# Second-layer weight blocks nine and ten of a fused attention and two-layer kernel: converted in other stretches of the program

## The chip, the cores and the metric

One core of a Trainium2 chip runs the whole program. The metric is the device time of an execution in microseconds (us). PE is the engine for matrix products, DVE the vector engine, ACT the engine for activation functions, POOL the general engine (GpSimd), and SP the engine whose queue issues nearly all DMA transfers.

## What is computed

Block-causal attention, a first layer with h - tanh(h), and a second, gated layer with a norm ahead of it, all in float32:

```python
attn = softmax(mask(q @ k.T / sqrt(64)))            # 4 x 8 heads x 576 x 64, blocks of 64
x = (attn @ v).transpose(0, 2, 1, 3).reshape(2304, 512)
h = x @ w_in                                        # 512 -> 2048
x = (h - tanh(h)) @ w_out                           # 2048 -> 512
xn = x / sqrt(mean(x * x) + 1e-6) * rms_g
g, val = xn @ w_gate, xn @ w_val                    # 512 -> 1536 each
out = (g / (1 + exp(-g)) * val) @ w_out2            # 1536 -> 512
```

## The kernel before, in words

The 2304 tokens are worked in six groups of 384. Attention and the first layer run interleaved, group by group (g = 0 to 5, 16 steps j each); the last group has no attention left, so its place beside the first layer is taken by preparing the second layer. The second layer then runs in three passes, each over a pair of groups. In a pass, `fast` (line 1095) goes through the 12 blocks j of the gate and value weights, 128 columns each. Per block PE forms seven products of six matmuls, in the order 1, 4, 5, 6, 0, 3, 2, so 42 matmuls; DVE adds and multiplies their results (lines 1112, 1113, 1115, 1117, 1121, 1122), ACT takes c (line 1111) and the silu (lines 1116, 1118), POOL one product (line 1119). Line 1121 takes product 2, the block's last. Then follow the products with the output weights.

Float32 numbers are multiplied as a high and a low part, each in a reduced format. So every weight block has to be **converted** before use (class `Convert`, line 776). A block's weights are two pieces (gate and value) of 512 KB. `load` brings a piece from memory into a staging tile `st` (SP); `piece` turns it into float32 in a tile `fu` (two ACT steps `cv`, `cu`, lines 141 and 143, and two DVE steps, lines 144 and 145; inputs arrive as float64 words). The seven weight combinations of the seven products are then made and split. The first half, combinations 0 to 2, is split as it stands: ACT writes the high part (line 803), DVE the low part (line 108), 768 columns. Four POOL sums (lines 794 to 798) then change `fu` in place, so they wait for the first split; then the second half, combinations 3 to 6, is split, 1024 columns. `fill` splits into `ws`, the tile that PE reads; `send` splits into a passing tile `wc` and stores it to memory (`w2d` for gate blocks, `wod` for output blocks). A block that was filled is stored too (`keep`), for passes two and three. `ws` has three buffers.

Where the blocks are converted: the six output blocks in groups three to five (g = 2 to 4), by a list of 24 items (`away`, line 828, four items a block) from which a number of items is taken after each step (line 996). In the last group a second list of 24 items: blocks 10, 0, 11, 1, 2 in full, of which 0, 1 and 2 stay in `ws`, and the two pieces of blocks 3 and 4. In pass one blocks 3 to 9 (`WHOLE`, line 52) are filled: 3 and 4 from their finished pieces, 5 to 9 from the start. In the loop over j, at block j the second half of block j + 1 is filled (line 1276), the first half of block j + 2 (line 1080, through `load_slot`), and the pieces of blocks j + 3 and j + 4 are converted (lines 1283 to 1286). Blocks 10 and 11 come back from `w2d` by a load, and in passes two and three all blocks do.

What sets the order: the PE queue is in the order in which the code is written. The order of DVE, ACT, POOL and SP is set by a scheduler when the program is built, up to the first block after `WHOLE`; from there on DVE, ACT and POOL too keep the written order (line 1273). Each engine works through its queue in that order.

Of the kernel before, what the change touches and what calls it, by code (L numbers as in the profile page):

```python
# [26 lines left out]
J1 = FF1 // 128  # L27
J2 = FF2 // 128
# [20 lines left out]

EARLY = 4  # L50
JH = J2 // 2
WHOLE = range(3, 10)
LAG = 2
SPLIT = 12
AVLEAD = 3
# [39 lines left out]
def build(ctx, tc, q, k, v, w_in, w_out, w_gate, w_val, w_out2, rms_g, ident_in, out):  # L95
# [496 lines left out]
    with tc.manual_schedule(engines={PE.engine}):  # L592
# [13 lines left out]
        class Both:  # L606
            n = 0
# [220 lines left out]
        def away(units, stay=(), raw=()):  # L828

            items = []  # L830
            fourth = None
            for n, c in enumerate(units):
                def first(n=n, c=c):
                    if n == 0:
                        c.load()
                    c.piece(0)
                    if n + 1 < len(units):
                        units[n + 1].load((0,))

                def second(n=n, c=c):  # L840
                    c.piece(1)
                    if n + 1 < len(units):
                        units[n + 1].load((1,))

                def third(c=c):
                    if c in stay:
                        c.fill(slot(c.j), 0)
                        return
                    c.send(0)
                    c.sums()  # L850

                def last(c=c):
                    if c in stay:
                        c.fill(slots[c.j], 1)
                    else:
                        c.send(1)
                items += [first, fourth, second] if fourth else [first, second]
                fourth = None
                if c not in raw:
                    items.append(third)  # L860
                    fourth = last
            return items + ([fourth] if fourth else [])
# [27 lines left out]
        def pair_x():  # L890
            return [[(wk if n == 0 else tp).tile([128, 4 if n < 3 else 2, TG], F32R, name=f"x{y}{n}",
                                                 tag=f"x{y}" if n == 0 else f"x{y}{n}") for y in "hl"] for n in range(4)]
# [16 lines left out]
        def slot(q):  # L909
            slots[q] = tp.tile([128, 2, 7, 256], F32R, name="ws", tag="ws", bufs=3)  # L910
            return slots[q]

        items = away([Convert("o", j) for j in range(JH)])
        x = None

        PREP = [(1, lambda: pair_load(0, 0)), (1, lambda: pair_load(0, 1)), (1, lambda: rms(0, 12)),
# [11 lines left out]
        for s in range(NSA):  # L928
            g, j = divmod(s, J1)
# [58 lines left out]
            if len(pend) > LAG:  # L988
                n = pend.pop(0)
# [3 lines left out]
                    out1(n, t)  # L993
                gts.pop(n)
            if 2 <= g < NG - 1:
                nit = {2: 0, 3: 5, 4: 13}[g] + max(j - 2, 0) * {2: 5, 3: 8, 4: 13}[g] // (J1 - 3)
                while 4 * JH - len(items) < min(nit, 4 * JH):
                    items.pop(0)()
            if j == J1 - 1:
                while att.pos < goal:  # L1000
                    att.step()
                if g == NG - 2:
                    mid.__exit__(None, None, None)
                    evm.__exit__(None, None, None)
                    cvs.__exit__(None, None, None)
                    x4.__exit__(None, None, None)
                    sat.close()
                    sw = ExitStack()
                    tp = sw.enter_context(tc.tile_pool(name="w2p", bufs=1, side="right"))
                    sw0 = ExitStack()  # L1010
                    env["cvp"] = sw0.enter_context(tc.tile_pool(name="w0", bufs=1, side="right"))
                    env["stg"] = sw0.enter_context(tc.tile_pool(name="st2", bufs=2, side="right"))
                    sev = ExitStack()
                    ev = sev.enter_context(tc.tile_pool(name="ev", bufs=3, side="right"))
                    space = tp.tile([128, 2, 7, 256], F32R, name="ws", tag="ws", bufs=3).bitcast(F32)
                    space = space.rearrange("p x n c -> p (x n c)")
                    env["x2s"] = lambda g, t: (space[:, DM * t:DM * t + DM] if g == NG - 2 else
                                               ev.tile([128, DM], F32, name="x2s", tag="x2s"))
                    x = pair_x()
                    wcp = sev.enter_context(tc.tile_pool(name="wcp", bufs=1, side="right"))  # L1020
                    env["wc"] = lambda: wcp.tile([128, 2, 4, 256], F32R, name="wc", tag="wc")
                    direct = [Convert("g", j) for j in range(J2)]
                    items = away([direct[n] for n in (10, 0, 11, 1, 2, 3, 4)], direct[0:3], direct[3:5])
            if g == NG - 1:
                for k, f in PREP:
                    if k == j:
# [46 lines left out]
        def load_slot(q):  # L1073
# [4 lines left out]
            if j < J2:  # L1078
                if p == 0 and j in WHOLE:
                    direct[j].fill(w, 0)  # L1080
# [189 lines left out]
        for p in range(NG // 2):  # L1270
            for j in range(J2):
                if p == 0 and j == WHOLE.stop:
                    ordered.enter_context(tc.manual_schedule(engines={DVE.engine, ACT.engine, POOL.engine}))
                if p == 0:
                    if j + 1 in WHOLE:
                        direct[j + 1].fill(slots[j + 1], 1)
                    if j + 1 < WHOLE.stop:
                        direct[j + 1].keep()
                if p or j:
                    load_slot(p * NQ + j + 2)  # L1280
                if p == 0:
                    if 5 <= j + 3 < WHOLE.stop:
                        direct[j + 3].piece(1)
                    if 5 <= j + 4 < WHOLE.stop:
                        direct[j + 4].load()
# [4 lines left out]
                for t in range(2):  # L1290
                    n = j - t - (8 if p == 0 else 7)
# [35 lines left out]
```

## Time and profile before

| | us |
|---|---|
| median of 3 runs | 1016.61 (1016.61 to 1017.07) |
| the profiled execution's own time | 1016.32 |
| its span, first to last instruction | 1014.5 |
| PE busy in the span | 1000.3 |
| first layer's last group ends, pass one begins | about 602 |
| the first-layer group before the last ends, staging of the last group begins | about 520 |

The span is read from its first to its last instruction; the execution's own time is 1.8 us more. [...] A matmul of 384 columns starts 0.17 us after the one ahead of it, though its row gives it about 0.34 us: matmuls overlap, so a busy PE can hide a gap of up to 0.17 us, and waits are read from one start to the next.

### The profile page before, as it was taken

The numbers are of one execution on the slowest core, as the hardware profiler recorded it, in microseconds if no ns is written. First come the engines' busy times: TensorE is split into PE (matmuls) and PEld (weight loads), VectorE is DVE, ScalarE is ACT, GpSimd is POOL, SyncE is SP. The second block draws the span as 40 slices with busy tenths as digits, with TensorE's granted clock in tenths as the row PEclk, the third lists the DMA queues.
The fourth block names the chain that finished last, engine by engine and source line by source line (L and its number), as shares of the span: only waits on it lengthen the run. The fifth ranks groups of instructions, "written<-read, shape, count | busy, mean of one in ns | idle before, by whom it ended". The sixth has DMA issues, their size and how long they took to land.

```text
span 1014.5 us, 17814 instructions
## 1 busy us (share of the span) xinstructions
PE 1000.3 (99%) x5983; PEld 921.8 (91%) x5983; DVE 705.6 (70%) x1497; ACT 659.5 (65%) x1530; POOL 341.9 (34%) x474
## 2 busy tenths in 40 slices
PE   8999999999999999999999999999999999999998
PEld 5766789999999999999899889999999999999998
DVE  6977867876777677687657887966854458644565
ACT  6978978887888778697858675635632247412253
POOL 5522112322323242434333424575121470111710
PEclk9999999999999999999999999999999999999999
DMA  9899959865787689867869998987796667876664
GB/s 225 252 352 341 282 170 263 270 195 143 207 252 206 181 241 287 231 204 240 301 208 363 377 345 317 353 310 278 278 350 254 249 228 257 298 284 233 257 219 156
DMA packets 185419, 265.22 MB, mean 261 GB/s; under 512 B 109040, under 2 KB 150384, under 8 KB 178032
## 3 DMA queue, kind: packets, MB, share of 16 engines
q1 hardware_dynamic: 184240, 263.69, 79.2%
q8 instruction: 47, 0.77, 0.3%
q10 hardware_dynamic: 1088, 0.39, 0.2%
q14 instruction: 44, 0.36, 0.1%
HBM read 201.65 MB, written 62.39 MB: 260 GB/s over the span
## 4 chain that ended last, share of the span: by engine, by line
PE 78%; DVE 6%; ACT 3%; issue 2%; POOL 2%; DMA 1%; SPq 0%; DVEq 0%; ACTq 0%; POOLq 0%
PE t L715 5%; PE t L717 5%; PE t L716 5%; PE gv L1064 5%; PE gv L1062 5%; PE t L481 5%; PE gv L1063 5%; PE acc L750 4%; PE acc L748 4%; PE acc L749 4%; PE t L525 3%; PE ga L1064 3%; PE ga L1062 3%; PE ga L1063 3%; PE ga L748 3%; PE ga L750 2%
## 5 line engine op out<-in xcount | busy, mean ns | idle before, releaser
L715 PE MATMUL t<-xh,w 128*128 128x384 f32 x384 | 138.6, 361 | 0.2
L717 PE MATMUL t<-xh,w 128*128 128x384 f32 x384 | 130.0, 339 | 0.4 <-DVE w L108 0.2
L716 PE MATMUL t<-xl,w 128*128 128x384 f32 x384 | 129.3, 337 | 0.0
L1064 PE MATMUL gv<-xh,ws 128*128 128x384 f32 x322 | 108.4, 337 | 3.2 <-DVE ws L108 3.2
L1062 PE MATMUL gv<-xh,ws 128*128 128x384 f32 x322 | 108.2, 336 | 0.2 <-DVE vb L1115 0.2
L1063 PE MATMUL gv<-xl,ws 128*128 128x384 f32 x322 | 108.1, 336 | 0.0
L748 PE MATMUL acc<-w,gh 128*128 128x512 f32 x252 | 102.5, 407 | 0.0
L750 PE MATMUL acc<-w,gl 128*128 128x512 f32 x252 | 99.7, 395 | 0.4 <-DVE gl L108 0.3
L749 PE MATMUL acc<-w,gh 128*128 128x512 f32 x252 | 99.2, 393 | 0.0
L1119 POOL TENSOR_TENSOR g<-va,vb 128x384 f32<-128x384 f32 x36 | 37.0, 1027 | 168.5 <-ACT va L1118 168.5
L496 ACT ACTIVATE pt<-pt,stat 128x64 f32<-128x64 f32 (+2 forms) x144 | 80.1, 557 | 18.7 <-DVE pt L494 17.2
L494 DVE TENSOR_SCALAR_CACHE_REDUCE pt<-t 128x64 f32<-128x64 f32 (+2 forms) x144 | 63.9, 450 | 18.4 <-PE t L481 17.2
L715 PEld LDWEIGHTS t<-xh,w 128*128 128x128 f32 x384 | 72.3, 188 | 4.6 <-issue 1.2
L716 PEld LDWEIGHTS t<-xl,w 128*128 128x128 f32 x384 | 72.5, 189 | 2.3 <-issue 0.5
L717 PEld LDWEIGHTS t<-xh,w 128*128 128x128 f32 x384 | 72.1, 188 | 1.0 <-DVE w L108 1.0
L108 DVE TENSOR_TENSOR gl<-gt,gh 128x384 fp32r<-128x384 f32 x84 | 57.5, 685 | 16.3 <-ACT gh L103 16.1
L980 DVE TENSOR_TENSOR gt<-t,gt 128x384 f32<-128x384 f32 x84 | 46.3, 551 | 31.2 <-ACT gt L974 30.9
L108 DVE TENSOR_TENSOR pp<-t,pp 128x512 fp32r<-128x512 f32 (+3 forms) x112 | 55.3, 507 | 15.8 <-ACT pp L103 14.9
L525 PE MATMUL t<-ident,pt 128*128 128x128 f32 x400 | 64.1, 273 | 2.2 <-POOL pt L510 2.1
L103 ACT ACTIVATE pp<-t 128x512 fp32r<-128x512 f32 (+5 forms) x144 | 60.2, 433 | 6.1 <-PE t L525 5.6
L1064 PEld LDWEIGHTS gv<-xh,ws 128*128 128x128 f32 x322 | 60.5, 188 | 3.8 <-DVE ws L108 3.8
L525 PEld LDWEIGHTS t<-ident,pt 128*128 128x128 f32 x400 | 49.9, 140 | 15.0 <-POOL pt L510 3.7
(196 smaller groups left out, 2959.9 us busy)
## 6 DMA issues: line engine op xcount, KB each, us to landing
ws<-w2d SPq DMA_DIRECT2D x26, 1792.0 KB, 7.8
ws<-wod SPq DMA_DIRECT2D x21, 1536.0 KB, 6.0
w<-w1d_i SPq DMA_DIRECT2D x60, 512.0 KB, 5.1
w<-w1d_o SPq DMA_DIRECT2D x48, 512.0 KB, 5.3
w2d<-ws SPq DMA_DIRECT2D x10, 1792.0 KB, 8.4
st<-in_moe_w_out SPq DMA_DIRECT2D x28, 512.0 KB, 6.1
st<-in_moe_w_in SPq DMA_DIRECT2D x16, 512.0 KB, 6.2
w1d_i<-w SPq DMA_DIRECT2D x16, 512.0 KB, 6.7
```

Source lines behind the costliest of these rows:

```text
L108: eng.tensor_tensor(out=o, in0=full, in1=hi.bitcast(F32), op=ALU.subtract)
L496: ACT.activation(out=pt[:, 0:keys], in_=pt[:, 0:keys], func=AF.Exp, scale=-1.0, bias=least, accum_out=st[:, 8 + ti:9 + ti])
L525: PE.transpose(t[:, (j - a) * 128:(j - a + 1) * 128], pt[:, j * 128:(j + 1) * 128], ident)
L715: PE.matmul(h, lhsT=wh[:, c], rhs=xh[:, kk], start=(kk == 0), stop=False)
L716: PE.matmul(h, lhsT=wh[:, c], rhs=xl[:, kk], start=False, stop=False)
L717: PE.matmul(h, lhsT=wl[:, c], rhs=xh[:, kk], start=False, stop=(kk == KD - 1))
L748: PE.matmul(acc, lhsT=gh[:, c], rhs=wh, start=first, stop=False, skip_group_check=more)
L749: PE.matmul(acc, lhsT=gh[:, c], rhs=wl, start=False, stop=False, skip_group_check=more)
L750: PE.matmul(acc, lhsT=gl[:, c], rhs=wh, start=False, stop=last, skip_group_check=more)
L1062: PE.matmul(ps, lhsT=wh[:, c], rhs=xh[:, kk], start=(first and kk == 0), stop=False, skip_group_check=more)
L1063: PE.matmul(ps, lhsT=wh[:, c], rhs=xl[:, kk], start=False, stop=False, skip_group_check=more)
L1064: PE.matmul(ps, lhsT=wl[:, c], rhs=xh[:, kk], start=False, stop=(last and kk == nk - 1), skip_group_check=more)
```

## The change

Block 10 becomes a seventh block of the first list: 28 items in groups three to five, with the numbers of items per step raised from 5, 13 and 24 at the groups' ends to 6, 15 and 28. The last group's list has block 9 in block 10's place. `WHOLE` ends at 8, so pass one converts blocks 5 to 8, and block 9 comes back from `w2d` by a load. The written order of DVE, ACT and POOL begins one block earlier.

```diff
-WHOLE = range(3, 10)
+WHOLE = range(3, 9)
...
-        items = away([Convert("o", j) for j in range(JH)])
+        direct = [Convert("g", j) for j in range(J2)]
+        items = away([Convert("o", j) for j in range(JH)] + direct[10:11])
+        nitems = len(items)
...
-                nit = {2: 0, 3: 5, 4: 13}[g] + max(j - 2, 0) * {2: 5, 3: 8, 4: 13}[g] // (J1 - 3)
-                while 4 * JH - len(items) < min(nit, 4 * JH):
+                nit = {2: 0, 3: 6, 4: 15}[g] + max(j - 2, 0) * {2: 6, 3: 9, 4: 13}[g] // (J1 - 3)
+                while nitems - len(items) < min(nit, nitems):
...
-                    direct = [Convert("g", j) for j in range(J2)]
-                    items = away([direct[n] for n in (10, 0, 11, 1, 2, 3, 4)], direct[0:3], direct[3:5])
+                    items = away([direct[n] for n in (9, 0, 11, 1, 2, 3, 4)], direct[0:3], direct[3:5])
```

The scheduler lays out the four free queues anew, and the rows that moved are not only those of blocks 9 and 10. Line numbers above 912 are one or two higher in the changed kernel (line 1121 becomes 1122, 1122 becomes 1123). `ws` of 768 columns is a first half's split, of 1024 a second half's; `g_3` and `g_4` are the results of blocks 3 and 4.

First place, SP where the last group begins. Before, from the last stores of the output blocks:

```order
L826 DMA wod<-wc 128x4x256 x2
L130 DMA st<-in_moe_w_gate 128x4x256
L130 DMA st<-in_moe_w_val 128x4x256
L869 DMA xn<-x2d 128x512
L870 DMA xn<-x2d 128x2x256
L869 DMA xn<-x2d 128x512
L870 DMA xn<-x2d 128x2x256
L684 DMA w_7041<-w1d_i_96 128x1024
```

Now, from the last such load of the first layer's weights:

```order
L694 DMA w_6742<-w1d_o_116 128x1024
L823 DMA w2d_82<-wc 256x1x768
L869 DMA xn<-x2d 128x512
L870 DMA xn<-x2d 128x2x256
L869 DMA xn<-x2d 128x512
L870 DMA xn<-x2d 128x2x256
L823 DMA w2d_82<-wc 256x1x1024
L684 DMA w_7070<-w1d_i_96 128x1024
L684 DMA w_7112<-w1d_i_95 128x1024
L130 DMA st<-in_moe_w_gate 128x4x256
L130 DMA st<-in_moe_w_val 128x4x256
```

The last group's first two staging loads stood ahead of the `xn` loads and now stand behind them, behind both stores of block 10 (`w2d_82`) and behind two loads of first-layer weights.

Second place, DVE from the end of the first layer into block 0 of pass one. Before:

```order
L771 RECIPROCAL rinv<-rinv 128x6
L1112 TENSOR_TENSOR va<-gv,c_7771 128x384
L144 TENSOR_SCALAR cv<-cv 128x512
L1113 TENSOR_TENSOR va<-gv,va 128x384
L145 SCALAR_TENSOR_TENSOR fu<-cv,cu 128x512
L1115 TENSOR_TENSOR vb<-gv,va 128x384
```

Now:

```order
L108 TENSOR_TENSOR ws<-fu,ws 128x768
L766 TENSOR_TENSOR x2s<-acc_7094,g_bc 128x512
L766 TENSOR_TENSOR x2s<-acc_7098,g_bc 128x512
L766 TENSOR_TENSOR x2s<-acc_7102,g_bc 128x512
L771 RECIPROCAL rinv<-rinv 128x6
L1113 TENSOR_TENSOR va<-gv,c_7800 128x384
L108 TENSOR_TENSOR ws<-fu,ws 128x1024
L1114 TENSOR_TENSOR va<-gv,va 128x384
L144 TENSOR_SCALAR cv<-cv 128x512
L1116 TENSOR_TENSOR vb<-gv,va 128x384
```

Both splits of block 2, which before stand well ahead of these rows, now stand around the first layer's last evacuations (`x2s`) and inside block 0's steps.

Third place, DVE around the end of blocks 3 and 4 of pass one, where the second halves of blocks 4 and 5 are split. Before, from block 4's first step:

```order
L1112 TENSOR_TENSOR va<-ga,c_8123 128x384
L144 TENSOR_SCALAR cv<-cv 128x512
L145 SCALAR_TENSOR_TENSOR fu<-cv,cu 128x512
L1113 TENSOR_TENSOR va<-ga,va 128x384
L144 TENSOR_SCALAR cv<-cv 128x512
L1115 TENSOR_TENSOR vb<-ga,va 128x384
L145 SCALAR_TENSOR_TENSOR fu<-cv,cu 128x512
L108 TENSOR_TENSOR ws<-fu,ws 128x1024
L1117 TENSOR_TENSOR va<-gv,va 128x384
L108 TENSOR_TENSOR ws<-fu,ws 128x768
L1121 TENSOR_TENSOR ga<-ga,va 128x384
L1122 TENSOR_TENSOR g_4_8184<-ga,gt 128x384
```

Now, the end of block 3 and, after the line of dots, the end of block 4:

```order
L1122 TENSOR_TENSOR gv<-gv,va 128x384
L144 TENSOR_SCALAR cv<-cv 128x512
L1123 TENSOR_TENSOR g_3_8123<-gv,gt 128x384
L145 SCALAR_TENSOR_TENSOR fu<-cv,cu 128x512
L108 TENSOR_TENSOR ws<-fu,ws 128x1024
L108 TENSOR_TENSOR ws<-fu,ws 128x768
...
L1118 TENSOR_TENSOR va<-gv,va 128x384
L144 TENSOR_SCALAR cv<-cv 128x512
L145 SCALAR_TENSOR_TENSOR fu<-cv,cu 128x512
L1122 TENSOR_TENSOR ga<-ga,va 128x384
L108 TENSOR_TENSOR ws<-fu,ws 128x1024
L1123 TENSOR_TENSOR g_4_8213<-ga,gt 128x384
```

Block 5's second half was split ahead of line 1117 of block 4 and now stands between block 4's last two steps; block 4's, which before follows block 2's last step, now follows block 3's. The second halves of blocks 3, 6 and 7 stand like block 5's, right behind line 1122; block 8's stands ahead of line 1122.

## Rows read from the trace of the kernel before

**Rows 1.** The page's head: the span, and each engine's busy time.

```profile
span 1014.5 us, 17814 instructions
PE 1000.3 (99%) x5983; PEld 921.8 (91%) x5983; DVE 705.6 (70%) x1497; ACT 659.5 (65%) x1530; POOL 341.9 (34%) x474
```

**Rows 2.** PE's waits: waiter, releaser: us in total, times, longest.

```profile
PE gv L1064 <- DVE ws L108: 3.2, 2, 1.7
...
PE t L550 <- DVE pp L108: 0.9, 1, 0.9
```

**Rows 3.** Busy us by stretch: length, PE, PEld, DVE, ACT, POOL, clock, DMA.

```profile
395.00:520.00 125.00, 124.13 (x696) 113.73 (x695) 91.20 (x188) 97.71 (x214) 50.59 (x70) 1.00 0.77 242
...
638.00:674.00 36.00, 32.80 (x187) 32.17 (x187) 32.07 (x49) 20.95 (x36) 17.88 (x22) 1.00 0.85 308
```

**Rows 4.** PE in order of time: start, duration, step, [idle before, releaser].

```profile
608.75 0.45 PE L1062 MATMUL gv<-xh,ws 128*128 128x384 f32 x1 [0.18 <-DVE vb L1115]
...
653.85 0.34 PE L1062 MATMUL gv<-xh,ws 128*128 128x384 f32 x1
...
655.08 0.34 PE L1063 MATMUL gv<-xl,ws 128*128 128x384 f32 x1
656.87 0.44 PE L1064 MATMUL gv<-xh,ws 128*128 128x384 f32 x1 [1.46 <-DVE ws L108]
...
666.20 0.44 PE L1064 MATMUL gv<-xh,ws 128*128 128x384 f32 x1 [1.74 <-DVE ws L108]
...
679.55 0.34 PE L1062 MATMUL gv<-xh,ws 128*128 128x384 f32 x1
```

**Rows 5.** DVE in order of time, pass one: splits and line 1121.

```profile
646.38 1.23 DVE L108 TENSOR_TENSOR ws<-fu,ws 128x1024 fp32r<-128x1024 f32 x1
647.52 0.56 DVE L1121 TENSOR_TENSOR gv<-gv,va 128x384 f32<-128x384 f32 x1
...
654.62 0.55 DVE L1121 TENSOR_TENSOR gv<-gv,va 128x384 f32<-128x384 f32 x1
655.08 1.74 DVE L108 TENSOR_TENSOR ws<-fu,ws 128x1024 fp32r<-128x1024 f32 x1
...
663.66 0.56 DVE L1121 TENSOR_TENSOR ga<-ga,va 128x384 f32<-128x384 f32 x1
664.13 2.02 DVE L108 TENSOR_TENSOR ws<-fu,ws 128x1024 fp32r<-128x1024 f32 x1
...
679.75 0.57 DVE L1121 TENSOR_TENSOR gv<-gv,va 128x384 f32<-128x384 f32 x1 [0.48 <-PE gv L1064]
```

**Rows 6.** DVE's costliest groups, 602 to 674 us: busy us, mean ns, idle before.

```profile
L108 DVE TENSOR_TENSOR ws<-fu,ws 128x1024 fp32r<-128x1024 f32 x7 | 9.9, 1408 | 0.1
L145 DVE SCALAR_TENSOR_TENSOR fu<-cv,cu 128x512 int32<-128x512 int32 x12 | 9.7, 809 | 0.6
L108 DVE TENSOR_TENSOR ws<-fu,ws 128x768 fp32r<-128x768 f32 x7 | 7.1, 1012 | 0.0
```

**Rows 7.** SP in order of time: staging, first-layer weights, the store of block 0.

```profile
523.13 0.37 SPq L130 DMA_DIRECT2D st<-in_moe_w_gate  x1
...
533.76 1.08 SPq L684 DMA_DIRECT2D w<-w1d_i  x1
...
599.11 0.62 SPq L815 DMA_DIRECT2D w2d<-ws  x1
```

**Rows 8.** POOL in order of time, pass one: sums and products.

```profile
649.48 0.74 POOL L794 TENSOR_TENSOR fu<-fu 128x256 f32<-128x256 f32 x1 [0.89 <-DVE ws L108]
...
654.73 1.01 POOL L1119 TENSOR_TENSOR g<-va,vb 128x384 f32<-128x384 f32 x1 [1.99 <-ACT va L1118]
...
664.07 1.00 POOL L1119 TENSOR_TENSOR g<-va,vb 128x384 f32<-128x384 f32 x1 [2.59 <-ACT va L1118]
```

**Rows 9.** The page's DMA issues: KB each, us from issue to landing.

```profile
w2d<-ws SPq DMA_DIRECT2D x10, 1792.0 KB, 8.4
```

**Rows 10.** ACT in order of time: the high part of a second half.

```profile
652.78 1.06 ACT L803 ACTIVATE ws<-fu 128x1024 fp32r<-128x1024 f32 x1 [0.32 <-POOL fu L798]
```

## The prediction

> **What bounds the kernel now.** The page's first section: PE is busy 1000.3 of 1014.5 us [rows 1]. Its matmuls overlap, so that figure hides short waits, but it shows what can be won at all: only what PE still waits for. The list of PE's waits says for what [rows 2]: the largest entry is 3.2 us, twice, for `ws`, the second layer's weights that DVE is still writing; the next one in the middle of the program is a single 0.9 us. The table of stretches places the two: from 638 to 674 us PE is busy 32.8 of 36 us and DVE 32.1, where DVE has 91.2 of 125 in the groups before [rows 3]. So in the first half of pass one DVE is the tight engine, and PE stops where DVE is late.
>
> PE's and DVE's order of time show the mechanism. A block starts at 653.85 and its matmuls follow each other every 0.17 us, 42 of them in 7.3 us. Number nine is the first that reads the low half of the block's second half. It should start 1.40 us after the block's start, at 655.25, and starts at 656.87: 1.62 us lost, of which the trace calls 1.46 idle. The next block loses the same way, 1.74 idle, so 1.90 [rows 4]. On DVE the split that PE needs (128x1024, line 108) stands both times right behind line 1121: 654.62 then 655.08, and 663.66 then 664.13. Line 1121 takes the last product of the block before, so it can't start until PE has begun the block that needs the split. Where the split stands ahead of line 1121, as at 646.38 with 1121 at 647.52, PE doesn't wait [rows 5]. That is how all seven blocks 3 to 9 fall out in the trace: five splits ahead of it or a block earlier and no wait, two behind it and two waits. **The place in DVE's queue decides, not the sum of DVE's work.**
>
> **What the change takes out.** Block nine leaves pass one. On DVE that is two conversions of 0.81 (line 145) and two splits of 1.01 and 1.41 us, 4.0 us in all without the two short clamps of line 144 [rows 6], a like chain on ACT and POOL, two loads and a store. If nothing else moved, DVE would come to the late splits of blocks 7 and 8 earlier by the two 0.8 us conversions that stand ahead of them, and by its splits, and both waits would go: -3.5 us, and nothing is late next, since the last split in before costs no wait.
>
> **What it puts in.** Block ten's conversion, another four items, goes to groups three to five. DVE and ACT have room there (DVE is busy 73% of 395 to 520 us [rows 3]), PE's waits there sum to one of 0.9 us [rows 2], and PE's order is the same. I take 0 for it; the bounds are -1 (that wait falls away) and +2 (two more like it). The last group has block nine where it had block ten: the same work. In pass one block nine's weights now come by a load of 1792 KB, issued some two blocks ahead; loads of that size have 14 us of cover, and I take 0.
>
> **What moves.** The last group's staging. Before, SP issues its first two loads at 523.13 [rows 7]. In the order of the change they stand behind both stores of block ten, four `xn` loads and two `w` loads, the second of which is issued at 533.76 in the trace of before [rows 7]: the conversions of the last group start about 10 us later. They work through the same list, so they also end later. Block two, finished before pass one in the old order, has its second split inside block 0's products in the new, and all of pass one's conversions run about a block behind. The order of DVE shows where that leaves the splits. The second halves of blocks 3, 5, 6 and 7 now stand right behind line 1122 (the old 1121), block 4's stands further back still, behind line 1123 and a conversion, and only block 8's stands ahead. **Two late places become five.**
>
> The price of one such place. The last product ends 0.20 us into the next block: the block at 679.55 has line 1121 at 679.75 [rows 4, 5]. 0.46 later the split can start, at best it takes 1.23 as at 646.38, and PE follows 0.05 after its end: 0.20 + 0.46 + 1.23 + 0.05 - 1.40 = 0.54 us is the least. At most it is what the two rows of before show, 1.62 and 1.90: there line 1121 itself was 0.57 late, since conversions stood ahead of it, and the split took 1.74 and 2.02 us [rows 5]. Beside these two splits POOL ran its product of line 1119, at 654.73 and 664.07 [rows 8].
>
> [...]
>
> Place by place:
> - Block 3: its pieces are early; it stands behind line 1122 with no conversion ahead, and ACT's silu, which feeds POOL's product, is queued behind the split's own half on ACT: 0.5. Its buffer is block 0's, and the store of block 0, issued at 599.11 before [rows 7], stands in the new order behind those of blocks 1 and 2. Such a store takes 8.4 us to land [rows 9]; if it is late, block 3 costs up to 2.4.
> - Block 4: line 1122, a clamp, line 1123 and a conversion stand ahead: 0.46 for a step of the products' kind and 0.81 for the conversion [rows 5, 6] more than the least, so 1.8 without the clamp. Its POOL sums come late too. I take 2.3, at most 3.
> - Block 5: two conversions around line 1118, as in the late places of before, but POOL's product behind the split: between 0.54 and 1.9, nearer to the upper since the conversions hold up line 1122 itself; 1.4.
> - Blocks 6 and 7: the order of their neighbours is that of before's blocks 7 and 8, row for row, one block earlier. I take the same, 1.6 and 1.9; at least 1.0 each.
> - Block 8: ahead of line 1122; 0.
>
> Sum 7.7 us, against 3.5 now.
>
> Block 0's own products. PE resumes there at 608.75, waiting for line 1115 [rows 4]. In the new order the second split of block 2 stands ahead of that step. It needs its first split, POOL's sums (649.48 to ACT's start at 652.78, 3.3 us), ACT's 1.06 and its own 1.22 [rows 8, 10]. No row shows when the first split ends there; if by 601, nothing is lost, if at 604, 2.4 us. I put it at 603, just ahead of the evacuations: +1.4.
>
> **Sum.** 7.7 - 3.5 + 1.4 + 0 = +5.6 us. The profiled execution took 1016.32 us (span 1014.5); +5.6 gives 1021.9. The median of the runs before is 0.29 above it, so **1022.0**, 0.5% slower.
>
> **The rivals.**
> *The waits go, as the description suggests* (-3.5, 1013.1). For it: less DVE work in the tight stretch. Against it: an engine's queue is followed in order, and a split's place right behind line 1122 costs 0.54 at least. It would need all conversions to be earlier than I read, which only block 8 shows. 0.08, together with smaller gains.
> *Cheap places* (four times 0.54 to 1.0, block 4 1.8 to 2.0, block 0 nothing to 0.5): 4.0 to 6.5 against 3.5, +0.5 to +3, about 1018. For it: DVE is given slack by every stall of PE, and POOL's product is queued behind some of the splits. Against it: the rows of before at the same order. It decides when line 1122 starts on time. About 0.22, two thirds of it within 0.2%.
> *The store of block 0 is late too*: block 3 2.4, block 0 2.4, the others at their upper ends, and a load for block 11 that waits behind the store of block 8: 2.4 + 2.4 + 3 + 1.9 + 1.6 + 1.9 = 13.2 against 3.5, +8 to +10, about 1025. The DMA engines are near full around 600 us, which speaks for it. 0.15.
> *Groups three to five* pay for block ten on PE (+2 at most) while pass one does as forecast; that stays inside the range.
>
> **Chances.** The forecast 0.55, cheap places 0.22, late store 0.15, a gain 0.08. The range, 1016.5 to 1026.5, leaves out the gain and part of the last. 0.2%, 2 us, is about what a measurement of this kernel can tell from no change: faster by more 0.07, within 0.16, slower 0.77.
>
> **What would show it.** Right: in the new profile PE's wait for `ws` written by DVE rises from twice to five times or so and from 3.2 to 6 to 8 us; each is at a block's ninth matmul, with line 1122 just before the split; DVE's first `cv` of the last group is at 540 us or later; PE waits for line 1116 in block 0. Wrong: fewer than four such waits, or waits of 0.4 each; the first staging of the last group still near 523; a new wait of several us in groups three to five, or at blocks 9 to 11 for their loads, which none of these terms holds.

## The result, and the profile after

The changed kernel takes 1026.64 us (median of 4 runs, 1024.93 to 1027.66), the kernel before 1016.61 beside it: ratio 1.0098, 95% interval 1.0082 to 1.0114, 10 us slower. The direction was forecast, the size was not: 1022.0 was expected, and the time lies 0.14 us above the range. The profiled execution, the fastest of the four, took 1024.93 us with a span of 1023.1, 8.6 more than before.

PE's waits in the changed kernel, first lines of the list (waiter, releaser: us in total, times, longest):

```profile
PE gv L1065 <- DVE ws L108: 3.9, 3, 1.7
PE ga L1065 <- DVE ws L108: 3.3, 2, 2.1
...
PE ga L1063 <- ACT ws L803: 1.2, 1, 1.2
...
PE ga L748 <- ACT va L103: 0.6, 1, 0.6
...
PE ga L750 <- DVE va L108: 0.5, 1, 0.5
PE gv L1063 <- DVE vb L1116: 0.4, 1, 0.4
```

Two waits of 3.2 us in all for `ws` [rows 2] have become five of 7.2, and one for ACT's half of a split. This is the forecast's mechanism. But the waits for `ws` and ACT grew by only 5.2 us, and the pass lost more. The stages, read from the starts of PE's products (the last column is from the last product of pass one's blocks to the first of pass two):

| | pass one begins | its 12 blocks | tail |
|---|---|---|---|
| before | 602.07 | 91.94 | 48.17 |
| after | 599.24 | 101.67 | 50.00 |

So +9.7 in the blocks, +1.8 in the tail, -2.8 ahead of pass one, -0.1 behind: 8.6. Of the 2.8, 1.1 us lie ahead of the third group, where the edit moves no instruction and executions differ by as much; without them the trace would give +9.8, near the 10 of the medians (an estimate). A block without a wait takes 7.32 us. Before, blocks 0, 7 and 8 take 0.54, 1.72 and 2.02 more; after, block 0 takes 0.72 more, block 3 0.68, block 4 6.65, block 5 2.02, block 6 1.45, block 7 2.01, block 8 none. Block 4 is the surprise. PE in order of time there (start, duration, step, idle before and releaser):

```profile
630.79 0.34 PE L1065 MATMUL gv<-xh,ws 128*128 128x384 f32 x1
632.31 0.44 PE L1063 MATMUL ga<-xh,ws 128*128 128x384 f32 x1 [1.18 <-ACT ws L803]
632.59 0.34 PE L1064 MATMUL ga<-xl,ws 128*128 128x384 f32 x1
635.07 0.69 PE L1065 MATMUL ga<-xh,ws 128*128 128x384 f32 x1 [2.14 <-DVE ws L108]
635.56 0.52 PE L1063 MATMUL ga<-xh,ws 128*128 128x384 f32 x1
635.88 0.52 PE L1064 MATMUL ga<-xl,ws 128*128 128x384 f32 x1
...
641.00 0.46 PE L1065 MATMUL gv<-xh,ws 128*128 128x384 f32 x1
641.29 0.34 PE L1063 MATMUL gv<-xh,ws 128*128 128x384 f32 x1
```

Two waits in a row (1.35 and 2.31 us from start to start), and then matmuls every 0.32 us instead of 0.174, with no wait between them, for six us. The table of stretches gives the reason in its clock column (length, PE, PEld, DVE, ACT, POOL, clock, DMA):

```profile
632.00:634.00 2.00, 0.62 (x2) 0.30 (x2) 2.00 (x5) 0.72 (x3) 0.53 (x1) 1.00 0.85 260
634.00:636.00 2.00, 0.93 (x3) 0.93 (x4) 1.88 (x2) 1.89 (x3) 0.04 (x1) 0.60 0.58 220
636.00:638.00 2.00, 2.00 (x8) 2.00 (x7) 0.56 (x1) 0.00 (x0) 1.84 (x3) 0.50 0.90 358
638.00:640.00 2.00, 2.00 (x7) 2.00 (x7) 0.56 (x1) 0.00 (x0) 1.05 (x2) 0.50 1.16 394
640.00:642.00 2.00, 2.00 (x10) 2.00 (x10) 1.30 (x3) 0.00 (x0) 0.00 (x0) 0.69 0.77 219
```

The granted clock of PE (TensorE), 1.00 in both stretches of [rows 3], falls to 0.50 in a stretch in which PE starts only two matmuls between those at 630.79 and 635.07. Of block 4's 6.65 us, 3.66 are the two waits and 2.99 this clock. PE counts as fully busy meanwhile, and no list of waits shows it.

The late places themselves, DVE and POOL in order of time (blocks 3, 5, 6 and 7 of the changed kernel):

```profile
622.15 0.56 DVE L1122 TENSOR_TENSOR ga<-ga,va 128x384 f32<-128x384 f32 x1
622.62 1.21 DVE L108 TENSOR_TENSOR ws<-fu,ws 128x1024 fp32r<-128x1024 f32 x1
...
645.12 2.01 DVE L108 TENSOR_TENSOR ws<-fu,ws 128x1024 fp32r<-128x1024 f32 x1
...
654.15 1.75 DVE L108 TENSOR_TENSOR ws<-fu,ws 128x1024 fp32r<-128x1024 f32 x1
...
663.23 2.02 DVE L108 TENSOR_TENSOR ws<-fu,ws 128x1024 fp32r<-128x1024 f32 x1
```

```profile
623.15 1.56 POOL L1120 TENSOR_TENSOR g<-va,vb 128x384 f32<-128x384 f32 x1 [2.98 <-ACT va L1119]
...
645.04 1.00 POOL L1120 TENSOR_TENSOR g<-va,vb 128x384 f32<-128x384 f32 x1 [5.91 <-ACT va L1119]
...
653.79 1.02 POOL L1120 TENSOR_TENSOR g<-va,vb 128x384 f32<-128x384 f32 x1 [1.99 <-ACT va L1119]
...
663.17 1.00 POOL L1120 TENSOR_TENSOR g<-va,vb 128x384 f32<-128x384 f32 x1 [2.60 <-ACT va L1119]
```

At these four places the one that starts first is not slowed. At block 3 the split starts first: it takes 1.21 and POOL's product 1.56 instead of 1.0. At the other three POOL starts first, by 0.06 to 0.36 us: its product takes 1.0 and the split 1.75 to 2.02. At block 5 the lead is 0.08 us only.

And the cause at the other end, SP in the last group: the first staging loads are at 535.94, where [rows 7] had 523.13.

```profile
528.83 0.56 SPq L823 DMA_DIRECT2D w2d<-wc  x1
529.49 2.91 SPq L684 DMA_DIRECT2D w<-w1d_i  x2
535.94 0.38 SPq L130 DMA_DIRECT2D st<-in_moe_w_gate  x1
```

### The profile page after: what moved, and what is told of

Read it like the earlier page. It is cut to its first block, busy times and chain, and to the rows that moved or that the text cites. A ratio compares the mean times of both kernels' runs of the same rounds, so it can differ in the third digit from the quotient of the medians.

```text
span 1023.1 us, 17817 instructions
## 1 busy us (share of the span) xinstructions
PE 1004.4 (98%) x5983; PEld 924.7 (90%) x5983; DVE 702.1 (69%) x1497; ACT 660.2 (65%) x1530; POOL 340.0 (33%) x474
## 4 chain that ended last, share of the span: by engine, by line
PE 79%; DMA 7%; DVE 7%; ACT 4%; issue 2%; POOL 1%; DVEq 0%; SPq 0%; ACTq 0%; POOLq 0%
PE t L481 5%; PE gv L1065 5%; PE gv L1063 5%; PE gv L1064 5%; PE t L715 5%; PE t L717 5%; PE t L716 5%; PE acc L748 4%; PE acc L750 4%; PE acc L749 4%; PE t L525 4%; PE ga L1065 3%; PE ga L1063 3%; PE ga L1064 3%; PE ga L750 2%; PE ga L748 2%
## 5 line engine op out<-in xcount | busy, mean ns | idle before, releaser
L108 DVE TENSOR_TENSOR gl<-gt,gh 128x384 fp32r<-128x384 f32 x84 | 55.3, 658 | 16.4 <-ACT gh L103 15.9
L1065 PE MATMUL ga<-xh,ws 128*128 128x384 f32 x182 | 62.5, 344 | 3.3 <-DVE ws L108 3.3
```

The lines of the kernel that those rows point to most:

```text
L108: eng.tensor_tensor(out=o, in0=full, in1=hi.bitcast(F32), op=ALU.subtract)
L1065: PE.matmul(ps, lhsT=wl[:, c], rhs=xh[:, kk], start=False, stop=(last and kk == nk - 1), skip_group_check=more)
```

## The experiments

Theory A: the delay of the last group's staging makes the late places, and a split's place in DVE's queue makes PE's wait. Rivals: the moved conversions themselves cost the time; or the weights' pieces are late whatever the place. Four tables of stages below hold what the traces gave. The start of pass one varies by some 1.5 us between profiled executions in groups where no instruction was moved (the first first-layer group takes 96.7 to 98.8 us), so costs are read from single stages.

**The delay alone.** The kernel before, its first list two steps slower, no block moved:

```diff
-                nit = {2: 0, 3: 5, 4: 13}[g] + max(j - 2, 0) * {2: 5, 3: 8, 4: 13}[g] // (J1 - 3)
+                nit = {2: 0, 3: 5, 4: 11}[g] + max(j - 2, 0) * {2: 5, 3: 6, 4: 13}[g] // (J1 - 3)
```

> The kernel before with one thing changed: the first list takes its items two steps later, so that the last group's first staging loads are issued some 12 us later, as in the changed kernel. No block is moved. In the order of DVE six second halves (blocks 3 to 8) then stand behind the block's last step, five of them as in the changed kernel. Theory A (the staging's delay makes the late places, and the moved conversions nothing): PE loses what the changed kernel loses at blocks 3 to 7 and the same 1.9 once more at block 8, about 1025 to 1029 us, with a stretch of TensorE at a granted clock of 0.50 behind block 4. Rival B (the block moved into groups three to five, or the shorter pass one, costs the time): within 2 us of the kernel before, 1015 to 1018.

1025.82 us, ratio 1.0099 (1.0085 to 1.0112): as large a loss as that of the whole change, without the change. That the totals are equal is in part chance: the delay alone loses 2.0 us at block 8, where the change loses none, and the change 1.8 us in its tail, where the delay alone loses none. First staging load at 536.92. PE's waits:

```profile
PE gv L1064 <- DVE ws L108: 5.6, 4, 1.7
...
PE ga L1064 <- DVE ws L108: 3.3, 2, 2.1
...
PE ga L1062 <- ACT ws L803: 1.2, 1, 1.2
```

| | pass one begins | its blocks | tail | lost in blocks 3, 4, 5, 6, 7, 8 |
|---|---|---|---|---|
| after | 599.24 | 101.67 | 50.00 | 0.68, 6.65, 2.02, 1.45, 2.01, 0 |
| delay alone | 600.13 | 102.32 | 48.22 | 0.68, 5.42, 2.01, 1.45, 2.04, 2.01 |

Six late places; those of blocks 3, 5, 6 and 7 are equal to a few hundredths. Block 4 has the same two waits (1.34 and 2.30 us) and a shorter slow stretch behind them, 1.8 us of loss instead of 3.0. It also begins pass one earlier than before, as the change does: the fifth group takes 98.1 us instead of 98.9 (after: 98.4), the last 67.0 instead of 67.4 (67.0), and from there to pass one 6.7 instead of 7.6 (6.7). So the delay gives back about 2 us ahead of pass one.

**The change without the delay.** Counts raised so that the list of 28 ends where that of 24 did:

```diff
-                nit = {2: 0, 3: 6, 4: 15}[g] + max(j - 2, 0) * {2: 6, 3: 9, 4: 13}[g] // (J1 - 3)
+                nit = {2: 0, 3: 7, 4: 17}[g] + max(j - 2, 0) * {2: 7, 3: 10, 4: 13}[g] // (J1 - 3)
```

> The changed kernel with the counts per step raised a little more (7, 17 and 28 at the groups' ends instead of 6, 15 and 28): the first list ends two steps earlier, as in the kernel before, and the last group's staging starts early again. Blocks nine and ten are where the change puts them. DVE's order then has one late place in pass one, block 7's. Theory A (the change loses by the staging's delay alone): the waits of blocks 3 to 6 and the slow clock behind block 4 go, one of 1.6 to 1.9 us stays where before had two; with up to 1.8 us in pass one's tail as in the changed kernel, 1013.5 to 1016.5. Rival B (block ten's conversion in groups three to five, or block nine's load, costs the time): 1020 or more.

First staging load at 523.43. One wait for `ws`, 1.5 us. 1017.41 us, ratio 1.0007 (0.9995 to 1.0019): nine of the ten us are gone, but the expected gain did not come.

**The removal alone**, with the counts of before:

```diff
-        items = away([Convert("o", j) for j in range(JH)] + direct[10:11])
+        items = away([Convert("o", j) for j in range(JH)])
...
-                SP.dma_start(out=w.bitcast(F32), in_=w2d[j])
+                SP.dma_start(out=w.bitcast(F32), in_=w2d[11 if j == 10 else j])
```

> The removal alone: block nine in the last group and out of pass one as in the change, block ten converted nowhere (left out: its place in pass one takes block eleven's weights), the first list and its counts as before. DVE's order from the last group on is that of the early-staging version. Theory A: within 1 us of that version, 1012.5 to 1016.5, since block ten's conversion in groups three to five is hidden (0, bounds -1 to +2). Rival B (it is not hidden): 2 us or more below that version.

1015.81 us, ratio 0.9988 (0.9978 to 0.9999), 1.9 us below the version with early staging by the ratios (1.6 by the medians; the intervals overlap a little): theory A's "within 1 us" fell here.

| | third group | fifth group | pass one begins | its blocks | tail |
|---|---|---|---|---|---|
| before | 102.55 | 98.85 | 602.07 | 91.94 | 48.17 |
| after (6, 15, 28) | 102.72 | 98.36 | 599.24 | 101.67 | 50.00 |
| early staging (7, 17, 28) | 103.72 | 99.61 | 602.39 | 90.36 | 50.18 |
| removal alone | 102.54 | 99.18 | 600.89 | 89.98 | 50.46 |

With seven items block ten costs 1.2 us in the third group (the other version with seven items has 103.74 there, the ones with six 102.7) and 0.4 in the fifth. With the change's own counts it cost 0.2 in the third, and the fifth was shorter. So for the change itself the term 0 holds, but only at its counts.

**Place against lateness.** The changed kernel, late staging kept, each second half's DVE split traced just ahead of line 1122, which is held behind it (`held` keeps two steps: that split, and the block's store, which has to follow it). The place, from the edit; the rest fills `held`:

```diff
-            DVE.tensor_tensor(lower, lower, u, ALU.add)
+            if held:
+                held.pop(0)()
+                pin(DVE.tensor_tensor(lower, lower, u, ALU.add))
+                held.pop(0)()
+            else:
+                DVE.tensor_tensor(lower, lower, u, ALU.add)
```

> The changed kernel with its late staging, but in pass one the DVE split of each second half is put ahead of the step that takes the block's last product, and that step is held behind it. Theory A (the place in DVE's queue decides, and the staging's delay is harmful by way of the place): the waits of blocks 3, 5, 6 and 7 go (0.57 + 1.89 + 1.32 + 1.90 = 5.7 us), block 4 keeps most of its own since its pieces come late too: 1020 to 1022. Rival B (the pieces are late whatever the place): the same waits within 0.5 us each, 1025 to 1028, since now the last step waits as well.

And the opposite, the list ended one step earlier (6, 16, 28) and all six splits held behind that step, again the place alone:

```diff
             DVE.tensor_tensor(lower, lower, u, ALU.add)
+            if held:
+                pin(held.pop(0)())
+                held.pop(0)()
```

> The opposite: the changed kernel with the first list finished one step of the first layer earlier, so that the staging starts as early as in the kernel before, and all of block 3 to 8's second-half splits held right behind the step that takes the block's last product. Theory A (place): six waits of 0.5 to 1.9 us, 0.5 where POOL's product starts behind the split and more where it starts first, 1016 to 1022. Rival B (lateness of the pieces): no such waits, 1011 to 1014.

| | blocks | lost in blocks 0, 3, 4, 5, 6, 7, 8 |
|---|---|---|
| after | 101.67 | 0.72, 0.68, 6.65, 2.02, 1.45, 2.01, 0 |
| splits ahead, late staging | 97.89 | 1.79, 0.21, 6.47, 0.33, 1.43, 0, 0 |
| splits behind, staging from 529.61 | 103.41 | 8.16, 1.28, 1.40, 1.80, 1.17, 0.64, 1.29 |

Splits ahead: 1023.11 us, ratio 1.0077 (1.0062 to 1.0091), 2 us better by the ratios, whose intervals overlap, where 1020 to 1022 was expected; the trace's blocks take 3.8 us less. The waits of blocks 3, 5 and 7 go. Holding the splits made the scheduler move conversions on DVE and steps on ACT and POOL too, so this run alone does not show that the place was the cause; the single swaps further down do. Block 6's wait changes its name only: PE now waits for line 1116's step. Block 4's stays, and its releaser is now ACT's high part: there the pieces are late. It is one wait now, and the clock falls behind it too:

```profile
637.59 0.69 PE L1066 MATMUL ga<-xh,ws 128*128 128x384 f32 x1 [2.85 <-ACT ws L803]
```

```profile
640.00:642.00 2.00, 2.00 (x8) 2.00 (x7) 2.00 (x6) 1.26 (x2) 1.65 (x2) 0.50 0.99 423
```

In the changed kernel block 4's chain can be followed back: POOL's last sum of that block ends at 631.12 and ACT's high part starts at 631.22; POOL could start at 627.86 only, behind the first half's split (626.83); and that stands on DVE behind the conversion at 625.10, which stands behind block 3's late split at 622.62. That reads as if one late place made the next one later, but it is not shown: with block 3's split ahead of its step, POOL's sums start 1.8 us ahead of block 4's first product, in the changed kernel 2.1.

Splits behind: 1029.04 us, ratio 1.0128 (1.0113 to 1.0142). The staging did not begin as early as was expected: 6.3 us ahead of the changed kernel's, 6.5 behind that of before. Each of the six places costs 0.54 to 1.29 us from one matmul's start to the next. The version with the same counts and no split behind such a step, further down, has its first staging load at 529.01 and loses 0.2 us in these six blocks, so the staging alone does not make these waits; conversions on DVE and ACT differ between the two as well. PE's waits here:

```profile
PE gv L1066 <- ACT c L1115: 5.6, 1, 5.6
PE gv L1068 <- DVE ws L805: 3.5, 4, 1.1
...
PE ga L1068 <- DVE ws L805: 1.6, 2, 1.1
```

The first line is why it lies above its expectation: block 0 waits 5.6 us. ACT's and DVE's queues hold conversions there whose loads were issued at 602.71 and later, and the clock is 0.50 from 610 to 616 us behind it.

A third version combined the early staging of the counts 7, 17 and 28 with splits ahead:

> Early staging (as in the version with counts 7, 17, 28) and, besides, the DVE split of each second half put ahead of the step that takes the block's last product, which is held behind it. No split of a second half stands late any more. Theory A (place): pass one's blocks have no wait for weights over 0.3 us, 1.6 to 1.9 us less than the version with early staging alone: 1012 to 1014.5. Rival B (the split ahead of the last step only shifts the wait to the step's bank): the same as the version with early staging alone within 0.5 us.

1020.54 us, ratio 1.0034 (1.0023 to 1.0045), blocks 93.34: neither theory. Holding the splits moved conversions in ACT's queue: the one whose load is issued at 627.94 now stands ahead of block 3's first silu, ACT waited 3.6 us for that load, and blocks 4, 5 and 6 lost 1.04, 3.19 and 0.95. The load itself is no later: with early staging alone it is issued at 627.29, as far behind the start of pass one, and its conversion stands further back, so nothing waits for it. The run tells nothing on the place.

**The clock.** The changed kernel with sixteen matmuls more ahead of block 4's waiting one:

```diff
+            ps4 = any_bank()[:, 0:TG]
+            if s == 4:
+                for n in range(16):
+                    PE.matmul(ps4, lhsT=w[:, 0, 1, 0:128], rhs=xa[0][:, 2], start=True, stop=True)
-            DVE.tensor_tensor(u, prod(4, xb, 1), c11, ALU.add)
+            DVE.tensor_tensor(u, prod(4, xb, 1, ps4, True), c11, ALU.add)
```

> The changed kernel with 16 more matmuls of 384 columns on PE in block 4, written ahead of its eighth matmul row's wait for the second half (their result is overwritten by the product that follows). DVE, ACT, POOL and SP keep their order. They take 16 x 0.17 = 2.8 us of a stretch in which PE waits for 4.3 us. Theory A (the slow matmuls from 635 to 641 us come from the fall of the granted clock to 0.50, and that from PE's idle stretch): the clock stays at 1.00 there, the 20 slow matmuls take 0.17 again and the time falls by about 2.9 us, to 1023 to 1024.5. Rival B (something else slows these matmuls, or the clock falls all the same): no change, 1026 to 1027.5; if PE was late already, up to 1 us slower.

PE at the same place, and the stretch after it:

```profile
631.90 2.98 PE L1116 MATMUL ga<-xh,ws 128*128 128x384 f32 x16
634.72 0.34 PE L1063 MATMUL ga<-xh,ws 128*128 128x384 f32 x1
634.89 0.34 PE L1064 MATMUL ga<-xl,ws 128*128 128x384 f32 x1
636.01 0.45 PE L1065 MATMUL ga<-xh,ws 128*128 128x384 f32 x1 [0.78 <-DVE ws L108]
636.29 0.34 PE L1063 MATMUL ga<-xh,ws 128*128 128x384 f32 x1
636.47 0.34 PE L1064 MATMUL ga<-xl,ws 128*128 128x384 f32 x1
```

```profile
636.00:638.00 2.00, 1.99 (x11) 1.99 (x12) 1.38 (x2) 0.83 (x2) 1.02 (x2) 1.00 0.80 326
638.00:640.00 2.00, 2.00 (x14) 2.00 (x13) 1.46 (x3) 0.00 (x0) 1.84 (x3) 1.00 0.88 366
```

The clock stays at 1.00 and the matmuls at 0.17. DVE, ACT, POOL and SP keep their order. Block 4 takes 11.20 us instead of 13.97: 2.8 us back for work that is thrown away, as expected. The time does not show it: 1024.76 us, ratio 1.0092 (1.0075 to 1.0109), just above the 1023 to 1024.5 expected and 0.6 us better by the ratios, whose intervals overlap. The 2.8 us are read from the trace alone.

**The tail.** The changed kernel with the written order beginning at block 10 again:

```diff
-                if p == 0 and j == WHOLE.stop:
+                if p == 0 and j == 10:
```

> The changed kernel with the written order of DVE, ACT and POOL beginning at block 10 again, not at block 9; nothing else differs, and DVE's order in blocks 0 to 8 is the same but for the first splits of a result. Theory A (the earlier begin of the written order makes the two new waits in pass one's tail, 0.8 and 0.6 us): the tail takes 48.2 us again instead of 50.0, and the time falls by 1 to 2 us, to 1024.5 to 1025.5. Rival B (the tail waits because of the load of block nine or of DVE's lateness in the blocks ahead): the tail stays at 50 us, 1026 to 1027.

Tail 48.22 instead of 50.00; 1024.21 us, ratio 1.0068 (1.0047 to 1.0090). All traces of this case agree: 50.0 to 50.5 in the seven versions with the written order from block 9, 48.2 to 48.3 in the seven with it from block 10. The cause is on POOL. In the changed kernel twelve sums of line 1128 stand in the written order ahead of block 10's product and three more ahead of block 11's; the first of the lines below is the first sum:

```profile
687.36 1.37 POOL L1128 TENSOR_TENSOR gs<-g,g 128x384 f32<-128x384 f32 x1
...
700.06 1.03 POOL L1120 TENSOR_TENSOR g<-va,vb 128x384 f32<-128x384 f32 x1
...
703.24 1.33 POOL L1128 TENSOR_TENSOR g<-g,g 128x384 f32<-128x384 f32 x1
704.53 1.01 POOL L1120 TENSOR_TENSOR g<-va,vb 128x384 f32<-128x384 f32 x1
```

Block 11's product ends at 705.54, and at 705.55 ACT starts the split that takes over the product's buffer `va`, for which PE waits. (ACT's row names a matmul of PE that ended at 705.51; by the rotation of the two `va` buffers it is POOL's product. That the written order makes the tail's waits, the edit shows; the way by POOL is read from the rows.) With the written order from block 10 on, the sums begin at 674.19 and that product stands at 702.48.

**A version that beats both?** First the change with both costs taken out (written order from block 10, counts 6, 17 and 28), then the same with one split moved, block 7's second half, ahead of line 1122 in block 6 as in the diff above:

> The blocks placed as in the change, the staging early, and the two costs found so far taken out: the written order of DVE, ACT and POOL begins at block 10 again (so no waits of 1.8 to 2 us in pass one's tail), and the counts are 6, 17 and 28 (so no seventh item per group three, which took 1 us there in the version with 7, 17 and 28). Theory A: the kernel before less one late place (1.9 us) and the rest unchanged, 1.5 to 2.5 us faster than it: ratio 0.9975 to 0.9985. Rival B (block ten in groups four and five costs what pass one gains): ratio 0.9990 to 1.0010.

> The version before this one with a single change in DVE's order: in block 6 the split of block 7's second half, which stood behind the step that takes the block's last product, stands just ahead of it; SP's order is the same. Theory A (the place alone makes the wait): block 7's loss of about 1.7 us goes to 0.3 or less and nothing takes its place, 1.4 to 1.9 us faster than the version with the split behind. Rival B (the pieces come too late for it, so that the held step now delays its bank, its buffer or the block's result): 0.5 us of gain or less.

| | fifth group | blocks | lost in block 7 | ratio to before |
|---|---|---|---|---|
| counts 6, 17, 28 | 102.09 | 90.12 | 1.75 | 1.0000 (0.9990 to 1.0011) |
| the same, block 7's split ahead | 102.13 | 89.16 | 0.74 | 0.9993 (0.9984 to 1.0002) |

The first did not gain: rival B. PE's waits in groups three to five, one of 0.9 us before, are now:

```profile
PE t L550 <- DVE pp L108: 1.6, 1, 1.6
PE t L525 <- DVE pp L108: 1.2, 1, 1.2
PE t L481 <- DVE pp L108: 0.9, 1, 0.9
```

The fifth group takes 102.1 us instead of 98.9, though it holds the same eleven items as with 7, 17 and 28 (99.6). What in the new order makes attention's split late was not tried. The second shows the place by itself, since block 7's split and line 1122 alone change sides in DVE's order and the queues of ACT, POOL and SP are the same: 1.0 us at block 7 in the trace, not the 1.4 to 1.9 expected (the ratios differ by 0.0007, and their intervals overlap). The split takes 1.21 again, ahead of POOL's product; the 0.63 that PE still waits is the lateness of the conversion that stands ahead of it on DVE.

Counts 6, 16 and 28, with no second half behind a last step:

> Counts 6, 16 and 28, which end the first list one step later than in the kernel before and one earlier than in the changed kernel, written order from block 10. The scheduler then puts no second half behind a block's last step, but four conversions ahead of block 0's first steps on ACT and DVE, behind staging loads that are issued only around the end of the first layer. Theory A (a place can also be harmful where a conversion waits for its load): no late wait in blocks 1 to 8, 3.5 us less than the kernel before, but 4 to 6 us at block 0, in all 0 to 3 us slower than the kernel before. Rival B (fewer late places is all that matters): 3 us faster than the kernel before.

1020.16 us, ratio 1.0037 (1.0023 to 1.0051). Blocks 3 to 8 lose 0.2 us in all and block 2 0.8, but block 0 8.1: 5.6 us of waiting for ACT's `c`, behind conversions whose loads come late, and a clock of 0.50 after it. As expected, somewhat dearer.

Last, the kernel before with its two late splits moved and nothing else (from the edit):

```diff
+                        env["hold"] = held if j in (6, 7) else None
                         direct[j + 1].fill(slots[j + 1], 1)
...
+            if held:
+                held.pop(0)()
+                pin(DVE.tensor_tensor(lower, lower, u, ALU.add))
+                held.pop(0)()
```

> The kernel before with its two late places swapped and nothing else: in blocks 6 and 7 the DVE split of the next block's second half stands just ahead of the step that takes the block's last product. SP's order is the same. Theory A (each swap is worth what it was worth at block 7 in the version with counts 6, 17 and 28, 1.0 us: the split starts ahead of POOL's product and no longer waits for the last product): pass one's blocks take 2 us less than 91.94, ratio 0.9975 to 0.9985. Rival B (DVE has no room there, and the held step delays the block's result and the next steps instead): ratio 0.9990 to 1.0010.

1013.41 us, ratio 0.9975 (0.9964 to 0.9985): 2.5 us faster than the kernel before and the best of all. Its blocks take 89.93 us, 2.01 less; in all four queues these two splits alone have changed their place. DVE and POOL at block 7's split:

```profile
653.66 1.21 DVE L805 TENSOR_TENSOR ws<-fu,ws 128x1024 fp32r<-128x1024 f32 x1
654.80 0.55 DVE L1126 TENSOR_TENSOR gv<-gv,va 128x384 f32<-128x384 f32 x1
```

```profile
653.78 1.97 POOL L1122 TENSOR_TENSOR g<-va,vb 128x384 f32<-128x384 f32 x1 [1.99 <-ACT va L1121]
```

The same two instructions as in [rows 5] and [rows 8], in the other order: the split takes 1.21 instead of 1.74, POOL's product 1.97 instead of 1.01, and nobody waits for POOL there. Block 7's wait goes from 1.62 to 0.62 us: the split takes 0.53 less, and it starts 0.47 earlier within the block, being no longer behind line 1121's step. Block 8's goes from 1.90 to 0.88. What is left is not the place: DVE comes late to both splits, from the conversions ahead of them.

## Why the prediction was right and where it failed

- **The mechanism and its cause** held. Five waits for DVE at blocks 3 to 7, each at the ninth matmul, the split behind line 1122 (block 4's behind line 1123 and a conversion), block 8 without one; the staging 12.8 us later (about 10 forecast). The delay alone gives the same waits at blocks 3, 5, 6 and 7 and nearly the same loss at block 4, and without it nine of ten us are gone. "The place in DVE's queue decides, not the sum of DVE's work" was too strong: the two swaps in the kernel before took out 1.0 us each of waits of 1.62 and 1.90, and the rest is DVE's lateness.
- **Blocks 3, 5, 6, 7**: 0.5, 1.4, 1.6 and 1.9 forecast, 0.57, 1.89, 1.32 and 1.90 measured from start to start, 5.7 for 5.4. That the sum fits is in part luck: block 5 was put too low, since POOL's product was expected behind the split and started 0.08 us ahead of it, and the split took 2.01 us. Block 6 was put too high. The terms of blocks 3 and 5 took it that a split ahead of POOL's product is not slowed, which no row of the forecast shows; block 3's split, 0.53 us ahead of it, took 1.21. Block 3's store was not late.
- **Block 4** was the failing step: 2.3 (at most 3) forecast, 6.65 measured. Two things were missing. The wait has two parts, ACT's high part (1.35) and DVE's low part (2.31), where the forecast had DVE's alone, at 1.8; the sentence "its POOL sums come late too" touched the first and was given 0.5 us, at most 1.2. And the clock: the prediction took matmuls at 0.17 us throughout, because the clock of before was 1.00 [rows 3], so a long stall was priced at its own length. The fall behind it cost another 3.0.
- **The written order's earlier begin** stood in the description of the change and got no term, without a reason. It costs 1.8 us in the tail, by way of POOL's queue.
- **Block 0**: +1.4 forecast, +0.2 measured. The term put the end of block 2's first split at 603, 0.9 us behind the start of pass one (602.07 before); it ended at 599.13, just ahead of that start (599.24). The second split then ended at 604.81, some 0.2 us late for the steps behind it.
- **Groups three to five and the last group** were put at 0 with a bound of -1. They took 1.7 us less, and with the delay alone 2.1 less, which hid the tail's cost in the total.
- **Loads of blocks 9 to 11**: 0 forecast; 0.4 at block 11.

In the sum: +5.6 forecast, +8.6 in the profiled execution. Block 4 +4.3 and the tail +1.8 are too little in it, block 0 1.2 and the stretch ahead of pass one 2.8 too much (1.1 of that where nothing was moved), so that errors both ways cancel in part. The last line of the forecast has a slip besides: 1016.61 and 5.6 give 1022.2, not 1022.0. The rival *cheap places* was out at once: only block 3's place was cheap. *The store of block 0 late* gave nearly the measured time for another reason, and is wrong: its two marks, 2.4 at block 3 and at block 0, are not there, though the DMA engines were near full, as it said (a mean busy share of 0.97 from 596 to 616 us in the trace of before).

## What to carry to other kernels

Look for the instruction that a moved block pushes back in a DMA queue, not only at the work moved: staging some 13 us later cost 10 us with no block moved at all, and the moved conversion 0.2 us in the third group at the change's own counts. When a split for the next block can stand on either side of a step that waits for PE, put it ahead, where its pieces are there by then (1.0 us a place in the two swaps); beside a neighbour on POOL, let the one start first that PE waits for (the split took 1.21 us instead of 1.74 in the one swap, 1.22 instead of 2.02 in the other). Move one instruction at a time: holding all splits at once moved other steps too, and in one of the two versions that held them ahead it lost more than it gained. And price a long wait, or two close together, higher than their sum: behind two of 1.35 and 2.31 us the granted clock was 0.50 here, which cost 3.0 us more in the changed kernel and 1.8 with the delay alone.

## What the runs showed of the hardware

After a stretch with few matmuls the granted clock fell to 0.50 within the program, and in block 4 of the changed kernel matmuls of 384 columns then started every 0.32 us instead of 0.17, for six us. It fell with two matmuls between 630.79 and 635.07 (that block), behind a single wait of 3.0 us (block 4 with the splits ahead, 2.85 of it idle), and behind one of 5.6 us (block 0 in the two versions with counts 6, 16 and 28). How long it stays low is not the same each time: behind the same two waits the changed kernel lost 3.0 us, the delay alone 1.8. Waits of 1.9 us between busy stretches left it at 1.00 (the changed kernel from 644 to 668 us, with those of blocks 5 and 7). In the filled version, where sixteen matmuls more stand in block 4's gap, it is 1.00 from 636 to 640, and so here the gap in PE's work made the fall. At what length of a gap the clock falls no run shows.

DVE's split and POOL's product slow each other where they run side by side, in both directions. Where DVE starts first, the split takes 1.21 to 1.23 us and POOL's product 1.33 to 1.97 (1.33 where it starts 0.76 us behind the split, beside block 8's split of the changed kernel; 1.97 at 0.12, in the first swap); where POOL does, by 0.06 to 0.36 us, its product takes 1.0 and the split 1.74 to 2.02. In the two late places of before the split took 0.51 and 0.79 us more than the 1.23 at 646.38 [rows 5], and 0.66 and 0.94 us of POOL's product were left when it started [rows 8]. The swaps agree: 1.21 for 1.74 and 1.22 for 2.02 where the split starts 0.1 to 0.2 us ahead of POOL's product. By what way the two slow each other no run shows.
